# An attention and MLP kernel: where the gates' low halves, the operands' differences, the summary rows and the last batch's accumulators stand in the order of work

## The chip, the cores and the metric

The kernel runs on one core of one Trainium2 chip. The metric is device time in microseconds (us) of one execution. The engines are named as in the profile: PE is TensorE (matrix products), PEld its weight loads, DVE is VectorE, ACT is ScalarE, POOL is GpSimd, SP is SyncE, whose queue issues the transfers. Each engine works through its own instructions strictly in the order in which they were written; engines wait for one another through semaphores, which are set by what an instruction reads and writes.

## The reference

Two stages, for four batches of 768 tokens. First an attention with 8 heads of 64 channels, in which each token sees the keys within 16 places of it and one summary per block of 32 keys (the maximum of the keys; the mean of the values):

```python
k_sum = k.reshape(B, H, nb, block, D).max(axis=3)
v_sum = v.reshape(B, H, nb, block, D).mean(axis=3)
scores_all = concat(where(mask_l, scale * q @ k.T, -1e9),
                    scale * q @ k_sum.T + log(block))
a = softmax(scores_all)
attn = a @ concat(v, v_sum)
```

Then, with x the attention's output (4 x 768 x 512), a low-rank mixing over the tokens and an MLP with 2048 hidden units:

```python
u = x + ((x.T @ U) @ V).T
out = u + max(u @ w_ch1, 0) @ w_ch2
```

Everything is float32 at the interface, and U, V and the two weights come as float64 words.

## The kernel before

**Tiles and exactness.** The products run in TensorE's float32r form. To keep precision a value is split into a high half (a cast) and a low half (value less high half), and a product is three matmuls: high by high, high by low, low by high. The helper `split` (lines 184 to 187) does this: the cast is ScalarE's (line 186), the subtraction that of the engine named (line 187), mostly GpSimd for weights and VectorE for what lies in PSUM. An accumulator is one PSUM bank of 128 x 512 float32, and all tiles in PSUM come from one pool of eight banks (`bank`, line 99), taken in turn: a new tile waits until the last reader of the bank's earlier tile is done.

**Stages.** A start-up does the attention and mixing of batch 0 in an order written out as a list of words (`START`). The *first stage* is the MLP of batch 0: 16 blocks `f` of 128 hidden units, each in two halves of the tokens, with `up` (line 919), a gate (`up_out`, lines 931 and 932) and `down_rows` (line 941). It also turns the weights from float64 words, splits them, sums them for the later batches, and stores these. Beside it runs the attention of batch 1, cut into steps (`one_bank_steps`) that are laid on *places*: `place(i)` is called four times per block (i = 4f to 4f + 3), the steps are spread from place 6 to 64, and the dictionary `later` puts loads and the first key maxima on places 0 to 21. In one half of a block the order is: gate, `place`, transfers, split of the weights, weight sums, the summing of values on GpSimd, the products `down_rows` of the half before, the next `place`.

Batches 1 to 3 have two phases each. The *up phase* (`up_phase`, line 1200) computes the hidden units of pairs of blocks from seven operand tiles, after the manner of Strassen and Winograd, in 54 steps and two more that run in the down phase. The *down phase* (`down_phase`, line 1295) has 16 rows `f`; a row is six tiles of output: four of 128 channels by 512 tokens (tiles 0 to 3), then two that hold two channel groups by the last 256 tokens (tiles 4 and 5), three matmuls per tile or group. The attention of the next batch is spread over both phases: `later_steps`, 15 steps over the up phase, the rest over steps 0 to 90 of the down phase, one about every 3.6 tiles.

**Gates.** Before row f of the down phase the hidden row must be made into its gate: the high half gh = relu(h) on ScalarE (line 1269), the low half gl on VectorE (line 1270), from gh. Both have two buffers, so gh of row f + 1 can only be written when TensorE has read row f - 1. `gates(st, f + 1)` stands ahead of row f's first tile; for row 0 it stands four steps ahead of the up phase's end.

**Weights of the later batches.** `fetch_weight` loads a pair of units (SP's queue), `prepare` casts one unit on ScalarE and makes its low half on GpSimd, four units ahead of use; four ticks (one per step) after the second unit of a pair is prepared, the next load into that buffer is issued. In the down phase `prepare` stands behind a row's last tile.

**Operands.** `operands(st, i, k)`, k = 0 to 3, makes the operand tiles from the mixed rows: `mix_u` leaves a 128 x 384 tile in PSUM (lines 705 and 713); ScalarE copies it to `st.x` (line 739, "kept"); for k = 1 to 3 the tile is split into a B operand (lines 186 and 187, low half on VectorE), VectorE makes one or two differences from it (line 749, tiles `tmp`), and these are split into T operands (low half on GpSimd).

**Other lines that are named.** `key_maxima`: a maximum on VectorE (line 319) and four small copies (line 336), on ScalarE for batch 1. `value_summaries`: two copies of 24 summary rows into the value tile (line 340). The sum that they copy is made on GpSimd (`add_vsum`, lines 261 to 275). `scores` (354) and `scores_by_subtiles` (377); exponentials (403 and 413); `square_values` (494), the product with the values; `normalise` (506 to 508), which frees that product's bank; `turn_half` (463, 457).

**The end.** `leave` (line 1316, VectorE) adds the residual rows to an accumulator and sends the result (line 1326). In the last batch the last two rows are put in the order tile by tile, row 14 and row 15 of a tile together, and each of the two channel groups in tiles 4 and 5 leaves by itself.

Of the kernel before, what the change touches and what calls it, by code (L numbers as in the profile page):

```python
# [13 lines left out]
ALU = mybir.AluOpType  # L14
# [72 lines left out]
def body(ctx: ExitStack, tc, q0, q1, k, v, vn, uv, w1, w2, mask, ident, rep, out):  # L87
# [515 lines left out]
    def one_bank_steps(st):  # L603
# [20 lines left out]
        def turn(h, a):  # L624
# [3 lines left out]
            if a == 1 and h >= 2:  # L628
                summaries(h - 1)
# [99 lines left out]
    def operands(st, i, k):  # L729
# [355 lines left out]
    def do(items):  # L1085
# [12 lines left out]
        4: lambda: key_maxima(nxt, 0),  # L1098
# [167 lines left out]
    def gates(st, f):  # L1266
        h = st.h[f // 2][:, f % 2]
        gh, gl = gate_place("gh"), gate_place("gl")
        nc.scalar.activation(gh, h, AF.Relu)  # L1269
        nc.vector.scalar_tensor_tensor(gl, h, 0.0, f32(gh), ALU.max, ALU.subtract)  # L1270
        return gh, gl

    def down_phase(st, g):
# [8 lines left out]
        acc, got = [], {}  # L1282
        for f, n in order:
            if f not in got:
                got[f] = (use_weight("down", f), *g)
                g = gates(st, f + 1) if f + 1 < NF else None
# [3 lines left out]
            q0, q1 = (0, DM) if n < NC else (DM, S)  # L1290
            channels = (n,) if n < NC else (2 * (n - NC), 2 * (n - NC) + 1)
            for i, c in enumerate(channels):
                place = acc[n][:, i * (q1 - q0) : (i + 1) * (q1 - q0)]
                for j, (part_w, gt) in enumerate(((0, gh), (0, gl), (1, gh))):
# [6 lines left out]
                        skip_group_check=n >= NC,  # L1301
                    )
                if f == NF - 1 and (n < NC or i == 1 or st.b == B - 1):
# [163 lines left out]
```

## Time and profile before

| what | value |
|---|---|
| time, median of 3 runs | 660.5 us (659.4 to 660.81) |
| time of the profiled execution | 661.57 us |
| its span | 659.8 us, granted clock 0.999 |
| TensorE busy | 636.1 us, 96% |
| TensorE weight loads busy | 571.1 us, 87% |
| VectorE, ScalarE, GpSimd busy | 362.5, 354.9, 364.2 us |
| moved by transfers | 116.17 MB, 176 GB/s in the mean |

How to read what follows. A row of the *timeline* has the start and the duration in us, engine, line, operation, output and input tiles, shapes and a count, and in brackets the idle time of the engine ahead of it and what ended that ("<-"). Rows with a count over 1 are merged: the duration then goes from the first start to the last end. The *table of waits* has who waited at which line for whom, the total in us, how often, and the longest. A wait "for issue" is one for which the profile shows no releaser. A *window* row has, for a stretch of time, the busy time of each engine, then the granted clock of TensorE, the busy share of the transfer engines and GB/s. Matmuls overlap one another, and the ends of matmuls are modelled. The start-up ends near 56 us, the first stage near 224; the up phases of batches 1, 2 and 3 begin near 224, 378 and 528, their down phases near 291, 442 and 585.

### The profile page before, as it was taken

What the parts mean: (1) busy time and instruction counts of PE and PEld (TensorE: products, weight loads), DVE (VectorE), ACT (ScalarE), POOL (GpSimd) and SP (SyncE); (2) the same over time, 40 slices, a digit from 0 to 9 for tenths busy, and PEclk for the clock granted to TensorE, in tenths of its full rate; (3) what the DMA queues carried; (4) which work ended last, traced back from release to release, by engine and by line L of the source; (5) the groups of instructions that cost most, each with busy time, mean ns of one, the idle gap of its engine ahead of it and who ended that gap; (6) DMA issues with size and microseconds to landing.
All of it is one profiled execution on the core that took longest, in us unless ns stands there. A gap on an engine that the chain in (4) does not pass through costs nothing.

```text
span 659.8 us, 14400 instructions
## 1 busy us (share of the span) xinstructions
PE 636.1 (96%) x5436; PEld 571.1 (87%) x5436; DVE 362.5 (55%) x996; ACT 354.9 (54%) x795; POOL 364.2 (55%) x402
## 2 busy tenths in 40 slices
PE   5899999999999999999999999999999999999997
PEld 5779878989888899998888899998888899998885
DVE  5679767765767596566553645566544522232223
ACT  4765666656564557665453467765553555553320
POOL 5423977975585776862245775771243565653320
PEclk9999999999999999999999999999999999999999
DMA  8996588776676169895519177886423164341102
GB/s 218 246 365 198 164 272 267 203 216 201 186 249 193 50 202 297 238 273 164 167 53 254 64 239 231 250 268 188 140 62 96 31 223 139 112 127 65 33 1 95
DMA packets 76358, 116.17 MB, mean 176 GB/s; under 512 B 6912, under 2 KB 51328, under 8 KB 76288
## 3 DMA queue, kind: packets, MB, share of 16 engines
q1 hardware_dynamic: 76288, 115.24, 58.0%
q8 instruction: 43, 0.70, 0.4%
q14 instruction: 27, 0.22, 0.1%
HBM read 91.10 MB, written 24.12 MB: 175 GB/s over the span
## 4 chain that ended last, share of the span: by engine, by line
PE 82%; DVE 5%; ACT 5%; DMA 3%; issue 2%; POOL 1%; SPq 1%; ACTq 0%; DVEq 0%; POOLq 0%
PE acc L1295 28%; PE ps_h L1200 26%; PE acc L941 8%; PE ps_h L919 7%; PE ps_x L494 3%; DMA place<-in_v 2%; PE ps_s L377 2%; PE ps_s L354 2%; DVE gl L1270 1%; PE ps_t L463 1%; PE ps_u L705 1%; PE ps_m L671 1%; ACT op L186 1%; DVE tmp L749 1%; PE ps_x L480 1%
## 5 line engine op out<-in xcount | busy, mean ns | idle before, releaser
L187 POOL TENSOR_TENSOR parts<-whole,parts 128x512 fp32r<-128x512 f32 (+1 forms) x144 | 182.4, 1274 | 151.3 <-ACT parts L186 143.2
L1295 PE MATMUL acc<-gh,parts 128*128 128x256 f32 (+1 forms) x768 | 199.1, 341 | 1.3 <-DVE o L1316 1.0
L1200 PE MATMUL ps_h<-op,parts 128*128 128x384 f32 x1008 | 181.6, 337 | 0.1
L1200 PEld LDWEIGHTS ps_h<-op,parts 128*128 128x128 f32 x1008 | 174.2, 188 | 2.7 <-issue 1.1
L1295 PEld LDWEIGHTS acc<-gh,parts 128*128 128x128 f32 x768 | 132.9, 189 | 19.5 <-issue 1.7
L1295 PE MATMUL acc<-gl,parts 128*128 128x256 f32 (+1 forms) x384 | 130.3, 339 | 1.8 <-DVE gl L1270 1.6
L1270 DVE SCALAR_TENSOR_TENSOR gl<-place,gh 128x768 fp32r<-128x768 f32 x48 | 58.9, 1226 | 101.6 <-ACT gh L1269 101.6
L186 ACT CAST parts<-whole 128x512 fp32r<-128x512 f32 (+1 forms) x144 | 83.1, 583 | 2.5 <-DMA whole<-up 1.2
L1295 PEld LDWEIGHTS acc<-gl,parts 128*128 128x128 f32 x384 | 72.7, 189 | 10.5 <-DVE gl L1270 3.8
L413 ACT ACTIVATE e<-e,neg 128x120 f32<-128x120 f32 x144 | 46.5, 386 | 61.3 <-DVE neg L403 61.3
L919 PE MATMUL ps_h<-place 128*128 128x384 f32 x384 | 74.3, 341 | 0.0
L941 PE MATMUL acc<-place,gh 128*128 128x512 f32 x192 | 67.4, 406 | 1.3 <-POOL place L187 1.1
L1269 ACT ACTIVATE gh<-place 128x768 fp32r<-128x768 f32 x48 | 40.5, 845 | 51.8 <-PE acc L1295 51.8
L919 PEld LDWEIGHTS ps_h<-place 128*128 128x128 f32 x384 | 66.1, 188 | 1.5 <-issue 0.4
L162 POOL TENSOR_SCALAR val<-place 128x512 f32<-128x512 f32 (+1 forms) x30 | 48.2, 1621 | 21.9 <-ACT place L149 18.2
L187 POOL TENSOR_TENSOR place<-val,place 128x512 fp32r<-128x512 f32 x29 | 38.8, 1360 | 21.3 <-ACT place L186 21.3
L187 POOL TENSOR_TENSOR op<-tmp,op 128x384 fp32r<-128x384 f32 x24 | 25.7, 1079 | 43.3 <-ACT op L186 42.9
L941 PEld LDWEIGHTS acc<-place,gh 128*128 128x128 f32 x192 | 35.8, 188 | 9.9 <-POOL place L187 2.9
L403 DVE CUSTOM_DVE_ANT_0 e<-ps_s,mask_sb 128x120 f32<-128x120 f32 x144 | 32.7, 276 | 10.4 <-PE ps_s L354 5.9
L941 PE MATMUL acc<-place,gl 128*128 128x512 f32 x96 | 37.7, 393 | 0.0
L932 DVE SCALAR_TENSOR_TENSOR gl<-ps_h,gh 128x384 fp32r<-128x384 f32 x32 | 17.8, 555 | 29.4 <-ACT gh L931 29.3
L931 ACT ACTIVATE gh<-ps_h 128x384 fp32r<-128x384 f32 x32 | 15.7, 492 | 32.2 <-PE ps_h L919 32.1
(118 smaller groups left out, 824.4 us busy)
## 6 DMA issues: line engine op xcount, KB each, us to landing
place<-in_w SPq DMA_DIRECT2D x32, 512.0 KB, 5.8
whole<-up SPq DMA_DIRECT2D x24, 512.0 KB, 4.2
whole<-down SPq DMA_DIRECT2D x24, 512.0 KB, 4.2
whole<-up SPq DMA_DIRECT2D x24, 384.0 KB, 3.5
vt<-in_v SPq DMA_DIRECT2D x48, 146.2 KB, 3.7
kt<-in_k SPq DMA_DIRECT2D x24, 288.0 KB, 5.3
there<-squares SPq DMA_DIRECT2D x16, 384.0 KB, 4.2
at<-there SPq DMA_DIRECT2D x64, 96.0 KB, 3.4
```

The source lines that it names most:

```text
L162: nc.gpsimd.tensor_scalar(f32(bits), f32(hi), 0.0, None, ALU.mult)
L186: nc.scalar.copy(hi, val)
L187: engine.tensor_tensor(lo, val, f32(hi), ALU.subtract)
L403: nc.vector.tensor_tensor_reduce(out=e[:, u, :], in0=ps[:, i * KC : (i + 1) * KC], in1=mask_sb[:, m, :], scale=-SCALE, scalar=BIG, op0=ALU ...
L413: nc.scalar.activation(e[:, u, :], e[:, u, :], AF.Exp, bias=st.neg[h][:, u : u + 1], scale=-1.0,)
L494: nc.tensor.matmul(ps[32 * i : 32 * i + 32, u * DV : (u + 1) * DV], at[:KC, i, u], vt[u % 2][:, (u // 2) * 2 + (i // 2 + u) % 2], start=Tr ...
L919: nc.tensor.matmul(ps[:, :NH], w_split[0, f][:, c % 2, part_w, c // 2], ut[:, c, :], start=(n == 0), stop=(n == 3 * NC - 1),)
L941: nc.tensor.matmul(acc[t], gt[:, sl], w_split[1, f][:, part_w], start=(first and j == 0), stop=(last and j == 2),)
L1200: nc.tensor.matmul(ps, a[:, sa, i], b[:, sb, i], start=(first and n == 0), stop=(n == 5), skip_group_check=not first,)
L1269: nc.scalar.activation(gh, h, AF.Relu)
L1270: nc.vector.scalar_tensor_tensor(gl, h, 0.0, f32(gh), ALU.max, ALU.subtract)
L1295: nc.tensor.matmul(place, w[:, part_w, c * P : (c + 1) * P], gt[:, q0:q1], start=(f == 0 and i == 0 and j == 0), stop=(f == NF - 1 and j = ...
```

## The change

- **Gates.** `gates` is cut into `gate_high` (ScalarE) and `gate_low` (VectorE). The high half of row f + 1 stays ahead of row f's first tile; the low half is issued behind row f's second tile, ahead of the step that follows that tile. For row 0 the high half is issued eight steps ahead of the up phase's end and the low half six.
- **Preparation.** `prepare` in the down phase stands behind a row's third tile instead of its last.
- **Accumulators.** In the last batch tiles 4 and 5 become four tiles of 128 x 256, each in its own bank, so that eight accumulators are open. Its last two rows are ordered as the four wide tiles of row 14, those of row 15, the narrow tiles of row 14, those of row 15. `leave` is called once per tile, with no half of a bank left out; in batches 1 and 2 it does what it did.
- **Operands.** For k = 1 to 3 the high half is cast before the copy to `st.x`, and VectorE makes the differences before the B operand's low half.
- **Batch 1 in the first stage.** The summary rows of head 0 are written after head 1's second turn (place 13) instead of after head 2's second half of scores (place 16); the key maxima of head 0 stand on place 5 instead of 4.

The diff, cut to its core:

```diff
@@ one_bank_steps
-            if h == 2:
-                summaries(0)
...
-            if a == 1 and h >= 2:
+            if a == 1 and h >= 1:
                 summaries(h - 1)
@@ operands
-        nc.scalar.copy(kept, ps.rearrange("p (u q) -> p u q", q=P))
+        def keep():
+            nc.scalar.copy(kept, ps.rearrange("p (u q) -> p u q", q=P))
+        def high(name, val):
+            nc.scalar.copy(st.op[name][:, 0, i], val)
+        def low(name, val, engine):
+            t = st.op[name][:, :, i]
+            engine.tensor_tensor(t[:, 1], val, f32(t[:, 0]), ALU.subtract)
         def part(name, val):
-            t = st.op[name][:, :, i]
-            split(t[:, 0], t[:, 1], val, nc.vector if name[0] == "B" else nc.gpsimd)
+            high(name, val)
+            low(name, val, nc.gpsimd)
...
         if k == 0:
+            keep()
             st.tmp["B12"] = kept
-        elif k == 1:
-            part("B22", ps)
+            return
+        name = (None, "B22", "B11", "B21")[k]
+        high(name, ps)
+        keep()
+        if k == 1:
             st.tmp["T3"] = tmp()
             combine(st.tmp["T3"], ps, st.tmp["B12"], ALU.subtract)
+            low(name, ps, nc.vector)
             part("T3", st.tmp["T3"])
         elif k == 2:
-            part("B11", ps)
             st.tmp["T1"] = tmp()
             st.tmp["T2"] = tmp()
             combine(st.tmp["T1"], st.tmp["B12"], ps, ALU.subtract)
             combine(st.tmp["T2"], st.tmp["T3"], ps, ALU.add)
+            low(name, ps, nc.vector)
             part("T1", st.tmp["T1"])
             part("T2", st.tmp["T2"])
         else:
-            part("B21", ps)
             combine(st.tmp["T3"], ps, st.tmp["T2"], ALU.subtract)
+            low(name, ps, nc.vector)
             part("T4", st.tmp["T3"])
@@ later
-        4: lambda: key_maxima(nxt, 0),
+        5: lambda: key_maxima(nxt, 0),
@@ gates
-    def gates(st, f):
+    def gate_high(st, f):
         h = st.h[f // 2][:, f % 2]
         gh, gl = gate_place("gh"), gate_place("gl")
         nc.scalar.activation(gh, h, AF.Relu)
+        return h, gh, gl
+    def gate_low(h, gh, gl):
         nc.vector.scalar_tensor_tensor(gl, h, 0.0, f32(gh), ALU.max, ALU.subtract)
-        return gh, gl
@@ down_phase
+        whole = [[(c, 0, DM)] for c in range(NC)]
+        rest = [(c, DM, S) for c in range(NC)]
+        tiles_of_out = whole + ([rest[:2], rest[2:]] if st.b < B - 1 else [[x] for x in rest])
+        n_all = len(tiles_of_out)
-        order = [(f, n) for f in range(NF) for n in range(NU)]
+        order = [(f, n) for f in range(NF) for n in range(n_all)]
         if st.b == B - 1:
-            order[-2 * NU :] = sorted(order[-2 * NU :], key=lambda fn: (fn[1], fn[0]))
+            order[-2 * n_all :] = sorted(order[-2 * n_all :], key=lambda fn: (fn[1] >= NC, fn))
...
-                got[f] = (use_weight("down", f), *g)
-                g = gates(st, f + 1) if f + 1 < NF else None
+                got[f], seen[f] = (use_weight("down", f), *g[1:]), 0
+                g = gate_high(st, f + 1) if f + 1 < NF else None
...
-                if f == NF - 1 and (n < NC or i == 1 or st.b == B - 1):
-                    leave(st, acc[n], q0, q1, channels[: i + 1] if st.b < B - 1 else (c,), i)
+            if f == NF - 1:
+                leave(st, acc[n], q0, q1, [c for c, _, _ in tiles_of_out[n]])
+            seen[f] += 1
+            if seen[f] == 2 and g:
+                gate_low(*g)
             yield
-            if n == NU - 1:
+            if seen[f] == 3:
                 prepare()
@@ the loop over the up phase
-            if i == UP - 4:
-                g = gates(cur, 0)
+            if i == UP - 8:
+                g = gate_high(cur, 0)
+            if i == UP - 6:
+                gate_low(*g)
```

More of the change, by code (lines that the diff above doesn't have):

```diff
@@ L1289, in down_phase @@
                 acc.append(bank(f"acc{n}"))
[L1290 to L1292 removed]
+            for i, (c, q0, q1) in enumerate(tiles_of_out[n]):
                 place = acc[n][:, i * (q1 - q0) : (i + 1) * (q1 - q0)]
@@ L1300, in down_phase, with leave @@
                         stop=(f == NF - 1 and j == 2),
-                        skip_group_check=n >= NC,
+                        skip_group_check=len(tiles_of_out[n]) > 1,
                     )
-                if f == NF - 1 and (n < NC or i == 1 or st.b == B - 1):
-                    leave(st, acc[n], q0, q1, channels[: i + 1] if st.b < B - 1 else (c,), i)
+            if f == NF - 1:
[3 more added lines that the diff above has]
+                gate_low(*g)
             yield
-            if n == NU - 1:
+            if seen[f] == 3:
                 prepare()
-    def leave(st, acc, q0, q1, channels, i):
+    def leave(st, acc, q0, q1, channels):
         n = len(channels)
-        first = 0 if n > 1 else i
         o = mo.tile([P, DM], F32, name="o", tag="val", bufs=VALS)[:, : n * (q1 - q0)]
@@ L1317, in leave @@
                 o[:, part].rearrange("p (u q) -> p u q", q=P),
-                acc[:, (first + k) * (q1 - q0) : (first + k + 1) * (q1 - q0)].rearrange(
-                    "p (u q) -> p u q", q=P
-                ),
+                acc[:, part].rearrange("p (u q) -> p u q", q=P),
                 channel_rows(st, c)[:, q0 // P : q1 // P],
```

2 lines of the change are left out of this document (1 added, 1 removed).

## The prediction

> **What bounds the kernel now.** I read the profile page first, then TensorE's table of waits, then the timeline of all engines around each wait. From the page:
>
> ```profile
> span 659.8 us, 14400 instructions
> PE 636.1 (96%) x5436; PEld 571.1 (87%) x5436; DVE 362.5 (55%) x996; ACT 354.9 (54%) x795; POOL 364.2 (55%) x402
> ```
>
> TensorE is busy for 636.1 of 659.8 us and no other engine for more than 56%. The change takes no matmul away and adds none, so it can only win time in which TensorE waits, or that lies behind its last matmul. Next, therefore, the waits of TensorE alone (line and what it waited for; total, times, longest in us). I leave out those of the start-up, which the diff does not touch:
>
> ```profile
> PE ps_s L377 <- issue: 2.1, 4, 0.7
> PE acc L1295 <- DVE gl L1270: 1.6, 3, 0.6
> PE ps_x L494 <- ACT vt L340: 1.4, 2, 1.2
> PE acc L941 <- POOL place L187: 1.1, 2, 0.7
> PE acc L1295 <- DVE o L1316: 1.0, 2, 0.5
> PE ps_u L705 <- DVE tmp L749: 0.7, 1, 0.7
> PE ps_t L463 <- DVE tmp L749: 0.5, 1, 0.5
> PE acc L1295 <- ACT gh L1269: 0.2, 1, 0.2
> ```
>
> They sum to 8.6 us, but each place costs more than is listed, because the end of a matmul is drawn later than the next one could have started. The timeline at one place:
>
> ```profile
> 67.45 0.40 PE L941 MATMUL acc<-place,gl 128*128 128x512 f32 x1
> 68.31 0.73 PE L941 MATMUL acc<-place,gh 128*128 128x512 f32 x2 [0.46 <-POOL place L187]
> 69.12 0.62 PE L941 MATMUL acc<-place,gh 128*128 128x512 f32 x2
> ```
>
> An undisturbed pair takes 0.62 and one matmul 0.40, so starts are 0.22 to 0.23 apart. The matmul after 67.45 could have started at 67.68; it started at 68.31, which is 0.63 and not 0.46, and its pair takes 0.73, another 0.11. So a wait costs its listed idle plus 0.17 + 0.11 = 0.28 us.
>
> **The first stage: key maxima one place later, the first summary rows sooner.** What stands around these waits on ScalarE, VectorE and GpSimd:
>
> ```profile
> 62.99 1.28 DVE L171 SCALAR_TENSOR_TENSOR val<-place,val 128x512 int32<-128x512 int32 x2
> 65.30 0.95 ACT L336 COPY kt<-km 64x48 f32<-64x48 f32 x4 [2.24 <-DVE km L319]
> 66.28 1.14 ACT L186 CAST place<-val 128x512 fp32r<-128x512 f32 x2
> 66.55 0.82 PE L354 MATMUL ps_s<-kt,qz 128*128 128x120 f32 x6
> 66.98 2.53 POOL L187 TENSOR_TENSOR place<-val,place 128x512 fp32r<-128x512 f32 x2 [4.24 <-ACT place L186]
> 78.29 3.05 POOL L187 TENSOR_TENSOR place<-val,place 128x512 fp32r<-128x512 f32 x2
> 85.58 0.37 POOL L275 TENSOR_SCALAR vsum<-vsum 128x64 f32<-128x64 f32 x1
> 89.19 0.49 ACT L931 ACTIVATE gh<-ps_h 128x384 fp32r<-128x384 f32 x1 [1.67 <-PE ps_h L919]
> 97.65 1.06 ACT L340 COPY vt<-vsum 24x390 f32<-24x390 f32 x2
> ```
>
> The weight's values were ready at 62.99 + 1.28 = 64.27, but its cast stood on ScalarE behind four copies of key maxima, which had waited 2.24 for VectorE. At place 5 the copies stand behind the casts, VectorE's order being the same (nothing of VectorE's is issued between the two places for an odd block). The casts start at 64.3 instead of 66.28, so GpSimd's low half starts 2.0 sooner, at 65.0, and its first half-weight (2.53 / 2) is there at 66.2, ahead of 67.68: the wait at 68.31 goes. GpSimd then runs without a pause up to the low halves of 78.29; a start 2.0 sooner there covers the second of the two waits (0.7 listed, 1.0 with what hides) and the 0.7 us by which TensorE itself comes sooner, with 0.3 left over. The price: the key copies now end near 65.4 + 0.95 = 66.4, against scores that started at 66.55. Cost 0, and at most a few tenths if the casts slip.
>
> The summary rows are written at 97.65 and TensorE waits for them (1.4). They now come right behind the copies of head 1's second turn, near 87.5 (where ScalarE's idle ahead of the gate at 89.19 begins, 89.19 - 1.67), and their sum on GpSimd is ready by then (85.58 + 0.37 = 85.95). If it were late, ScalarE's gate at 89.19 and all behind it would wait; ScalarE idles 1.67 ahead of that gate, which covers the 1.06 of the copies. Saved: 1.1 + 1.4 listed at three places, + 3 x 0.28 = **3.3 us**.
>
> **Operands: differences ahead of low halves, the kept rows behind the high half.** Around the longest of these waits:
>
> ```profile
> 217.59 0.48 ACT L186 CAST op<-ps_u 128x384 fp32r<-128x384 f32 x1
> 218.10 0.56 DVE L187 TENSOR_TENSOR op<-ps_u,op 128x384 fp32r<-128x384 f32 x1 [1.86 <-ACT op L186]
> 219.04 0.55 DVE L749 TENSOR_TENSOR tmp<-tmp,ps_u 128x384 f32<-128x384 f32 x1
> ```
>
> TensorE next needs this PSUM bank, and its last reader ends at 219.59. Everything depends on whether VectorE may read the bank while ScalarE still does. If it may, the differences start with the first cast, the last read ends about 1 us sooner, and both waits for L749 go: 0.7 + 0.5 + 2 x 0.28 = 1.8 us. If not, VectorE starts where it does now (ScalarE's two reads only change places), runs the same two or three operations in another order and ends where it does now: 0. The trace has no two engines on one bank at once: VectorE's 218.10 follows the cast's end, 218.07, though there it needs its data. The Trainium skill, "PSUM — Partial Sum Buffer", section "PSUM bank collisions raise a hardware error", says that two engines must not touch one bank and quadrant at a time, reads against reads included, and that scheduling adds a dependency; by it the 1.8 us stay. The nearest row is the table's "DVE o L1316": TensorE waits there for VectorE's read of the other half of a bank, other addresses altogether. I take **0** and keep 1.8 for the range. Sure is only that the T operands are there one VectorE operation (about 0.5) sooner, which helps ScalarE's queue, next.
>
> **The gates and the weights' preparation in batches 1 and 2.** Two kinds of wait:
>
> ```profile
> 312.56 1.41 DVE L1270 SCALAR_TENSOR_TENSOR gl<-place,gh 128x768 fp32r<-128x768 f32 x1 [1.76 <-ACT gh L1269]
> 313.89 0.15 DVE L506 TENSOR_SCALAR sum<-ps_x 128x6 f32<-128x6 f32 x1
> 314.30 0.56 DVE L508 TENSOR_TENSOR x<-ps_x,sum 128x384 f32<-128x384 f32 x1
> 371.28 0.62 ACT L186 CAST parts<-whole 128x512 fp32r<-128x512 f32 x1
> 371.81 0.84 ACT L1269 ACTIVATE gh<-place 128x768 fp32r<-128x768 f32 x1
> ```
>
> At 312.56 VectorE has waited 1.76 for the gate's high half and then works 1.41, with the normalisation behind it in its queue. The scores that "waited for issue" (2.1) come just after that normalisation ends (314.30 + 0.56 = 314.86): they wait for the bank that it frees. Two of the four products stand right behind their row's first tile, and there the normalisation now precedes the low half: about 2 us sooner against a wait of 1.0. The other two stand behind the second tile, still behind the low half; there it helps that the weight's cast (0.62) no longer stands ahead of the gate on ScalarE, 0.5 against a listed 0.3. The waits for gl outside the tail go likewise: at 371.81 the gate loses the 0.53 in front of it, and 0.5 from the operands, against a listed 0.6 and 0.28. Saved: 2.1 + two thirds of 1.6 = 3.2 listed at six places, + 6 x 0.28 = 4.9.
>
> What is added: the low half now waits behind whatever VectorE does after the first tile, and TensorE needs it one row later. The tightest place has an operand step there:
>
> ```profile
> 343.90 2.01 DVE L1270 SCALAR_TENSOR_TENSOR gl<-place,gh 128x768 fp32r<-128x768 f32 x1 [0.32 <-ACT gh L1269]
> 344.54 0.48 ACT L186 CAST op<-ps_u 128x384 fp32r<-128x384 f32 x1
> 347.70 0.40 PE L1295 MATMUL acc<-gl,parts 128*128 128x512 f32 x1
> L1270 DVE SCALAR_TENSOR_TENSOR gl<-place,gh x48: 916/1112/2016, 290.0 to 646.5; 128x768 fp32r<-128x768 f32 x48
> ```
>
> ScalarE's reads end at 345.0, two VectorE operations of 0.55 at about 346.1; then gl, 0.92 (the shortest of 48, by the row of its line) to 2.01, ends between 347.0 and 348.1 against 347.70. Lost: 0 to 0.4 + 0.28, once in each of two batches, 0 to 1.4. I take 0.5, so **4.4 us** net. The preparation moved three steps up issues a cast, GpSimd's low half and, four ticks later, a load on SP's queue, ahead of outputs and later loads there. Its weight is used four rows later, about 4 x 4.2 = 17 us by the spacings below, so I cost it 0; were GpSimd 2 us late, SP would hold that load and what follows by as much. The gate of row 0 moved four up-steps sooner has no wait now: 0.
>
> **The tail.** Eight accumulators let the last two rows run as four whole tiles, four whole tiles, then the narrow ones, each in its own bank:
>
> ```profile
> 645.30 0.52 PE L1295 MATMUL acc<-gh,parts 128*128 128x256 f32 x2
> 656.48 0.29 PE L1295 MATMUL acc<-gh,parts 128*128 128x256 f32 x1
> 656.80 0.42 DVE L1316 TENSOR_TENSOR o<-acc,x 128x256 f32<-128x256 f32 x1 [0.72 <-PE acc L1295]
> out_t<-o SPq DMA_DIRECT2D x4, 128.0 KB, 1.7
> 654.00:655.00 1.00, 1.00 (x9) 1.00 (x10) 0.41 (x1) 0.00 (x0) 0.00 (x0) 1.00 0.85 321
> ```
>
> Row 14 starts at 645.30 + 0.52 - 0.40 = 645.42. Unbroken, its and row 15's 24 wide matmuls take 24 x 0.228 and the 24 narrow ones 24 x 0.12 (0.40 for a pair less 0.28): 8.35, so the last starts at 645.42 + 8.35 - 0.12 = 653.65 instead of 656.48, 2.8 sooner. Row 15 starts 2.7 behind row 14 instead of 0.7, time enough for its gate (0.84 as at 371.81, + 0.92 to 1.11); and the waits for gh, gl and o leave (0.2 + 0.5 + 1.0 + 4 x 0.28 = 2.8, the same by the other way). Narrow tiles end 0.36 apart and VectorE takes 0.42 for one, partly overlapped: up to 0.2 late. Outputs come at 256 KB per 3 x 0.228 us, 380 GB/s, where a busy microsecond shows 321: up to 0.5 late. At row 0 the eighth bank waits for the last sum of the up phase; its cover is three narrow steps of 0.36 against 0.32 + 0.55, at most a few tenths. I take **2.8**, lower end 2.0.
>
> **Sum.** 3.3 + 0 + 4.4 + 2.8 = 10.5 us. The profiled run took 661.57 (span 659.8 and 1.8 around it): 651.1. It is 1.1 above the median of the three runs shown, 660.5, against which the result is held: **650.0 us**.
>
> **Rivals.** (1) Both engines read a bank at once and the operands' waits go too: 648.2. For it: the two engines would only read. Against: the wait for L1316 and the page. (2) The first stage gives its gain back: GpSimd is busy there almost without a pause, and a sooner TensorE may meet the next low half instead. Then 653.3. For it: only 0.3 us were left over in the sum above. Against: TensorE's list has two such waits in all, so behind the second GpSimd keeps up by itself. (3) The waits are only replaced, each by the next late engine, and the tail alone is won: 657.7. Against: GpSimd, VectorE and ScalarE are each 55% busy. (4) Slower: the clock. TensorE without its pauses might be granted less than now. Each 1% costs 6.4 us of the 636, so from 1.65% on all is eaten; at 0.97 it would be 669. Against it stands the last up phase, where TensorE and its weight loads leave no gap and the clock is full:
>
> ```profile
> 550.00:560.00 10.00, 10.00 (x60) 10.00 (x59) 2.22 (x4) 4.97 (x11) 5.87 (x5) 1.00 0.50 147
> ```
>
> **How the numbers follow.** My forecast 0.60, (1) 0.15, (2) 0.15, (3) 0.06, (4) 0.04. The range: low, (1) with the 0.5 for the low half not lost and 1 us of scatter like that of the three runs (659.4 to 660.81), 646.5; high, (2) with half of the batches' gain, 653.3 + 2.4 = 655.7, taken as 655.5. A change under 0.2%, 1.3 us, can't be told from none. Only (4), and a failure of (3) in the tail as well, are not faster: faster 0.94, same 0.03, slower 0.03.
>
> **What would show it.** Right: TensorE's table of waits without "DVE o", "ACT gh", "POOL place" and "ACT vt", with "DVE tmp" still there; narrow L1316 some 0.36 apart at the end; the low halves without their idle on VectorE in batches 1 and 2. Wrong: L377 still waiting after a product, new waits for gl near the operand steps, or a clock under 0.99.

## The result, and the profile after

The changed kernel takes 649.99 us in the median (648.68 to 651.52) against 660.31 us (659.4 to 660.81) of the kernel before, measured beside it: a ratio of 0.9846, 95% interval 0.9821 to 0.9871, or 10.3 us less. The profiled execution took 649.63 us with a span of 647.8 and a granted clock of 1.0. First the page: the span, TensorE's and the other engines' busy times, and the shares of the chain that ended last.

```profile
span 647.8 us, 14395 instructions
PE 631.3 (97%) x5436; PEld 570.0 (88%) x5436; DVE 360.7 (56%) x996; ACT 356.2 (55%) x795; POOL 364.6 (56%) x402
PE 91%; DMA 4%; DVE 2%; ACT 2%; issue 1%; SPq 0%; DVEq 0%; ACTq 0%
```

The same 5436 matmuls are done, and VectorE, ScalarE and GpSimd have as much to do as before within 2 us. TensorE's 4.8 us less of "busy" are no less work either: 14 waits have left its table, and with each goes the 0.28 by which the ends around a wait are drawn late, an estimated 3.9 of the 4.8. What went is waiting. TensorE's table of waits, whole (what it waited for; total, times, longest):

```profile
PE ps_s L354 <- DVE place L336: 8.0, 1, 8.0
PE ps_s L354 <- DMA place<-in_q: 1.6, 1, 1.6
PE ps_n L293 <- DMA place<-in_v: 1.0, 2, 0.6
PE ps_t L463 <- DVE op L746: 0.7, 1, 0.7
PE ps_m L669 <- issue: 0.6, 1, 0.6
PE ps_u L703 <- DVE op L746: 0.5, 1, 0.5
PE ps_s L354 <- POOL place L340: 0.4, 1, 0.4
```

Behind the start-up only two are left, those of lines 463 and 703. They are the two waits for an operand's bank. Together they are as long as before, but that of line 463 was 0.5 and is 0.7, and the other was 0.7 and is 0.5. They have a new last reader: the B operand's low half (line 746) now reads the bank last, where a difference did.

How much was won where can be read from the starts of the matmuls, which are not modelled: both kernels issue 5436, so the n-th of one is set against the n-th of the other. Both begin at 8.01; the last starts at 656.48 before and at 644.14 after, 12.34 sooner. Cut at the 700th matmul (64 us), the 2200th (260 us, in batch 1's up phase), the 4800th (543 us, in batch 3's) and the last 48, the gain is

| stretch | changed kernel | forecast |
|---|---|---|
| start-up | 0.67 | 0 |
| first stage | 3.67 | 3.3 |
| batches 1 and 2 | 4.95 | 4.4 |
| batch 3 up to the last 48 matmuls | 0.21 | 0 |
| last 48 matmuls | 2.84 | 2.8 |

From 12.34, 0.34 is lost again behind the last matmul (656.48 to the span's end at 659.8 before, 644.14 to 647.8 after). The start-up, which the diff does not touch, is scatter: over the thirteen changed kernels of this study it ended between 1.77 later and 1.51 sooner than in the profiled run of before. The waits for first loads differ there (1.6 for `in_q` in the table above), and in three runs (gates and preparation alone, order alone, changed without the gates' split) the granted clock is 0.72 to 0.76 between 33 and 39 us, where it is 1.00 before. The profiled run of before was also 0.6 to 1.3 above the medians of its kernel (660.31 to 660.99), so that 11.9 us between the two profiled runs go with 10.3 between the medians.

The stages, in the changed kernel's timeline. The first stage:

```profile
63.69 1.14 ACT L186 CAST place<-val 128x512 fp32r<-128x512 f32 x2 [1.31 <-DVE val L171]
64.39 2.98 POOL L187 TENSOR_TENSOR place<-val,place 128x512 fp32r<-128x512 f32 x2 [2.33 <-ACT place L186]
64.74 0.95 ACT L336 COPY kt<-km 64x48 f32<-64x48 f32 x4
...
83.12 0.37 POOL L275 TENSOR_SCALAR vsum<-vsum 128x64 f32<-128x64 f32 x1
85.30 1.05 ACT L340 COPY vt<-vsum 24x390 f32<-24x390 f32 x2
```

The casts run ahead of the key copies, GpSimd's low half starts at 64.39 instead of 66.98, and the summary rows are written at 85.30, behind a sum that was ready at 83.49. An operand step:

```profile
169.21 0.47 ACT L742 CAST op<-ps_u 128x384 fp32r<-128x384 f32 x1
169.58 0.49 ACT L739 COPY x<-ps_u 128x384 f32<-128x384 f32 x1
170.16 0.55 DVE L756 TENSOR_TENSOR tmp<-x,ps_u 128x384 f32<-128x384 f32 x1 [1.61 <-ACT x L739]
...
171.09 0.55 DVE L746 TENSOR_TENSOR op<-ps_u,op 128x384 fp32r<-128x384 f32 x1
...
171.79 0.52 PE L463 MATMUL ps_t<-ident_sb,e 128*120 128x128 f32 x3 [0.70 <-DVE op L746]
...
175.82 0.56 DVE L756 TENSOR_TENSOR tmp<-ps_u,tmp 128x384 f32<-128x384 f32 x1 [1.47 <-ACT x L739]
```

VectorE's difference starts behind ScalarE's second read, the copy to `st.x`. At 170.16 its other input is an earlier row of that same tile `x`, so that this row alone does not show what it waits for. At 175.82 its inputs are the bank and a `tmp` that VectorE itself made at 170.63, and still it waits for the copy: only the bank is left to order the two. A product in batch 1, then the tail:

```profile
306.35 0.17 DVE L506 TENSOR_SCALAR sum<-ps_x 128x6 f32<-128x6 f32 x1 [1.58 <-PE ps_x L494]
...
308.14 1.94 DVE L1285 SCALAR_TENSOR_TENSOR gl<-place,gh 128x768 fp32r<-128x768 f32 x1
309.13 0.85 PE L377 MATMUL ps_s<-kt,qz 64*64 64x120 f32 x24
...
639.54 2.73 DVE L1336 TENSOR_TENSOR o<-acc,x 128x512 f32<-128x512 f32 x4 [1.59 <-PE acc L1313]
643.38 1.50 DVE L1336 TENSOR_TENSOR o<-acc,x 128x256 f32<-128x256 f32 x4 [1.10 <-PE acc L1313]
644.14 0.28 PE L1313 MATMUL acc<-gh,parts 128*128 128x256 f32 x1
```

The normalisation precedes the low half, and line 377's 24 matmuls run without a break. At the end four sums take 1.50, so they start (1.50 - 0.42) / 3 = 0.36 apart, each right behind its tile.

### The profile page after: what moved, and what is told of

It is laid out like the page before. It is cut to its first block, busy times and chain, and to the rows that moved or that the text cites. A ratio compares the mean times of both kernels' runs of the same rounds, so it can differ in the third digit from the quotient of the medians.

```text
span 647.8 us, 14395 instructions
## 1 busy us (share of the span) xinstructions
PE 631.3 (97%) x5436; PEld 570.0 (88%) x5436; DVE 360.7 (56%) x996; ACT 356.2 (55%) x795; POOL 364.6 (56%) x402
## 4 chain that ended last, share of the span: by engine, by line
PE 91%; DMA 4%; DVE 2%; ACT 2%; issue 1%; SPq 0%; DVEq 0%; ACTq 0%
PE acc L1313 31%; PE ps_h L1212 27%; PE acc L953 10%; PE ps_h L931 9%; PE ps_x L494 3%; PE ps_s L354 3%; PE ps_s L377 2%; DMA place<-in_q 2%; PE ps_u L703 2%; DMA qz<-in_q 1%; PE ps_t L463 1%; PE ps_m L669 1%; PE ps_u L711 1%; PE ps_x L480 1%; PE ps_r L687 1%
## 5 line engine op out<-in xcount | busy, mean ns | idle before, releaser
L1285 DVE SCALAR_TENSOR_TENSOR gl<-place,gh 128x768 fp32r<-128x768 f32 x48 | 55.2, 1149 | 71.5 <-ACT gh L1281 71.4
L168 DVE SCALAR_TENSOR_TENSOR val<-place,val 128x512 int32<-128x512 int32 (+1 forms) x33 | 32.0, 972 | 3.1 <-POOL val L162 3.0
L1238 DVE TENSOR_TENSOR place<-place,ps_h 128x384 f32<-128x384 f32 x24 | 13.2, 550 | 36.8 <-PE ps_h L1212 36.8
```

The costliest lines, as they stand in the source:

```text
L168: lambda lo, hi, bits: nc.vector.scalar_tensor_tensor(bits, lo, 29, bits, ALU.logical_shift_right, ALU.bitwise_or),
```

## The experiments

The same cut of the matmuls' starts, for every kernel run; gains in us against the profiled run of before, behind the start-up. A stretch that a kernel leaves as it was differs by up to 0.23, nearly all of it at one matmul of the first stage (90.34 in the kernel before). In two runs one transfer came late in batch 1: TensorE's tables have "ps_x L494 <- DMA at<-there" with 0.4 in the tail alone and 0.7 in the order alone, which is their -0.32 and -0.75.

| run | ratio, 95% interval | first stage | batches 1, 2 | batch 3 | last 48 |
|---|---|---|---|---|---|
| tail alone | 0.9962 [0.9948, 0.9976] | 0.23 | -0.32 | 0.02 | 2.84 |
| first stage alone | 0.9943 [0.9925, 0.9960] | 3.39 | 0.03 | -0.01 | -0.04 |
| gates and preparation alone | 0.9942 [0.9922, 0.9962] | 0.19 | 3.17 | 0.21 | -0.02 |
| operands alone | 0.9964 [0.9951, 0.9977] | 0.24 | 1.73 | 0.00 | -0.01 |
| order alone | 0.9986 [0.9972, 0.9999] | 0.23 | -0.75 | 0.00 | 1.29 |
| low half alone | 0.9974 [0.9963, 0.9985] | 0.19 | 1.91 | 0.21 | -0.02 |
| preparation alone | 0.9953 [0.9935, 0.9971] | 0.03 | 3.11 | 0.00 | 0.00 |
| key maxima alone | 0.9975 [0.9959, 0.9991] | 1.70 | -0.03 | 0.00 | 0.00 |
| changed, without the gates' split | 0.9853 [0.9830, 0.9876] | 3.67 | 5.01 | -0.01 | 2.84 |
| changed, all reads from the copy | 0.9853 [0.9836, 0.9870] | 4.05 | 4.07 | 0.21 | 2.84 |
| changed, cast and low half from the copy | 0.9804 [0.9783, 0.9826] | 5.43 | 5.39 | 0.21 | 2.84 |
| changed, cast from the copy | 0.9797 [0.9774, 0.9819] | 4.77 | 5.71 | 0.21 | 2.84 |

The four parts alone sum to 2.77 + 3.37 + 3.55 + 1.96 = 11.65 us in these starts, the whole change has 3.67 + 4.95 + 0.21 + 2.84 = 11.67: what is won is kept to the end.

In batches 1 and 2, though, two parts overlap, and that their sums agree is a coincidence. By the starts around each place, the whole change wins 3.22 there at the four waits of line 377, 0.95 at the two listed waits for gl (373.85 and 524.31 in the kernel before), and 0.74 at two more waits for gl (337.64 and 488.12) that are listed on the weight load alone. The first of these, in the kernel before:

```profile
337.64 0.19 PEld L1295 LDWEIGHTS acc<-gl,parts 128*128 128x128 f32 x1 [0.47 <-DVE gl L1270]
```

Gates and preparation alone win the 3.22 and the 0.74, and lose 0.84 at four places that wait for gl. The operands alone win 0.99 at the listed waits for gl and the same hidden ones, 0.78. So the hidden gain is counted twice, and a loss that comes only without the operands' new order makes up for it.

**The tail alone.** Eight accumulators and the new order of the last two rows, nothing else.

```diff
-            order[-2 * NU :] = sorted(order[-2 * NU :], key=lambda fn: (fn[1], fn[0]))
+            order[-2 * n_all :] = sorted(order[-2 * n_all :], key=lambda fn: (fn[1] >= NC, fn))
...
+            for i, (c, q0, q1) in enumerate(tiles_of_out[n]):
```

> Only the eight accumulators and the order of the last two rows; the rest as before. Theory of own waits (each part takes away its own waits and TensorE keeps the time): 2.8 us less, ratio 0.9958; the waits for gh, gl and o behind 645 us are gone, the last two rows take 8.35 us from first to last start, the narrow sums stand 0.36 to 0.42 apart. Rival (the outputs are the bound at the end): the last matmul comes 2.8 sooner but the span ends 2.0 sooner or less.

The last 48 matmuls come 2.84 sooner, and the waits for gh, for o and for gl in the tail are gone. The 2.8 of the forecast is the gain up to the last matmul; 0.4 of it goes again behind it (the span, 657.3, ends 3.7 behind the last matmul's start instead of 3.3).

**The first stage alone.**

```diff
-            if h == 2:
-                summaries(0)
...
-            if a == 1 and h >= 2:
+            if a == 1 and h >= 1:
...
-        4: lambda: key_maxima(nxt, 0),
+        5: lambda: key_maxima(nxt, 0),
```

> Only the key maxima at place 5 and the first summary rows at place 13. Own waits: 3.3 us less, ratio 0.995; the waits of TensorE for L187 and L340 are gone from its table and those for L749 stand. Rival (the first stage gives it back, GpSimd being busy there without a pause): 0.7 to 1.5 us less, with a new wait for a low half of L187 between 75 and 130 us.

3.39 in the first stage, and nothing of it is given back in the batches (0.03, -0.01, -0.04).

**Gates and preparation alone.** The low half is issued behind a row's second tile, but behind the first tile of row 14 in the last batch, where the old order of the tail needs it.

```diff
-                g = gates(st, f + 1) if f + 1 < NF else None
+                g = gate_high(st, f + 1) if f + 1 < NF else None
...
+            if seen[f] == (1 if st.b == B - 1 and f == NF - 2 else 2) and g:
+                gate_low(*g)
...
-            if n == NU - 1:
+            if seen[f] == 3:
                 prepare()
```

> Only the gates' two halves issued apart, row 0 four steps sooner, and the preparation behind the third tile; for the last batch's row 15 the low half is issued behind row 14's first tile, since the tail's order is still the old one. Own waits: 4.0 to 4.9 us less, ratio 0.993; the scores no longer wait for issue, the waits for gl outside the tail nearly gone. Rival (the low half now comes late behind the operand steps): 2.5 us less or fewer, with waits for gl at the rows that have an operand step.

The waits of line 377 are gone, and batches 1 and 2 win 3.17 us in all. But the waits for gl in batches 1 and 2, which the forecast counted here, stay and grow. TensorE's table of this run, and one of those places:

```profile
PE acc L1298 <- DVE gl L1273: 2.0, 3, 0.8
```

```profile
369.89 2.00 POOL L187 TENSOR_TENSOR op<-tmp,op 128x384 fp32r<-128x384 f32 x2 [0.60 <-ACT op L186]
370.18 0.84 ACT L1269 ACTIVATE gh<-place 128x768 fp32r<-128x768 f32 x1
371.05 1.65 DVE L1273 SCALAR_TENSOR_TENSOR gl<-place,gh 128x768 fp32r<-128x768 f32 x1 [1.33 <-ACT gh L1269]
```

The gate does come sooner, since no weight's cast stands ahead of it; but the low half now runs beside GpSimd's low halves of the T operands and takes 1.65, where the shortest of its kind takes 0.92. The preparation alone has the same 2.0 in its table and the low half alone 1.5, so it is the preparation's move that lengthens these waits.

**Operands alone.**

```diff
+        high(name, ps)
+        keep()
+        if k == 1:
             st.tmp["T3"] = tmp()
             combine(st.tmp["T3"], ps, st.tmp["B12"], ALU.subtract)
+            low(name, ps, nc.vector)
             part("T3", st.tmp["T3"])
```

> Only the operands: high half ahead of the kept copy, differences ahead of low halves. Reads of one bank by two engines one after the other: the differences begin when ScalarE's second read ends, TensorE's two waits for VectorE (0.7 and 0.5) stay, only named after the low half instead of the difference; 0 to 0.9 us less, from gates that stand 0.5 sooner on ScalarE at the end of two batches. Reads side by side: the differences begin with the cast, both waits go, 1.8 to 2.7 us less.

Both bank waits stay, 0.7 at line 463 and 0.5 at line 705, with the low half as their last reader, and still 1.73 us are won in batches 1 and 2. Of the waits for gl in TensorE's table only the tail's is left (0.5, once): the T operands are cast one VectorE operation sooner, and with them the gate behind them in ScalarE's queue. This is the forecast's "one VectorE operation (about 0.5) sooner, which helps ScalarE's queue". Each of the two listed waits gives 0.48 and 0.51, less than listed idle plus 0.28, because some 0.4 of it stays on the weight load; the two hidden ones give 0.39 each. The 0.24 in the first stage belongs to the operands too: -0.24 and 0.29 at the two bank waits and 0.18 at one place between.

**All reads from the copy.** The changed kernel with ScalarE's copy to `st.x` first; cast, differences and low half then all read this copy, and the bank has one reader.

```diff
+        keep(ps)
+        ps = kept
         high(name, ps)
-        keep()
```

> The changed kernel, and ScalarE's copy to x comes first; high halves, differences and low halves then read that copy instead of the PSUM bank, so the bank has one reader, 0.48 us. Reads of one bank go one after the other, and TensorE waits for the bank: its two waits behind the operands (0.7 and 0.5, with 0.28 each 1.8) go, 8.5 to 12 us less than before in all. Rival: VectorE's operations now have both inputs in SBUF and are slowed beside GpSimd, as gl is (0.92 alone, up to 2.0); operations of 0.55 take up to 1.1, the T operands and the gates behind them come later, new waits for gl; no gain on the changed kernel or a loss of up to 1 us.

Both waits at the bank go, which shows that the readers one after another were what held it. But the time is that of the changed kernel. From TensorE's table of this run, then its timeline at a step like the one shown above:

```profile
PE ps_h L932 <- DVE gl L945: 1.1, 1, 1.1
PE acc L1314 <- DVE gl L1286: 1.1, 2, 0.6
```

```profile
167.75 2.85 POOL L187 TENSOR_TENSOR place<-val,place 128x512 fp32r<-128x512 f32 x2 [1.05 <-ACT place L186]
...
169.38 1.64 DVE L756 TENSOR_TENSOR tmp<-tmp,x 128x384 f32<-128x384 f32 x1
```

The difference, 0.55 long with one input in PSUM, takes 1.64 with both in SBUF: it ends at 171.02, 0.42 behind GpSimd's low halves (167.75 + 2.85 = 170.60), as if it had been let through only then. VectorE falls behind, and new waits for gl take what the bank gave. The Trainium skill, "SBUF — State Buffer", section "SBUF: two separate sides", says that a VectorE operation with two inputs in SBUF and a GpSimd operation share a pair of ports, when the GpSimd operation reads SBUF as well, and that the one that comes second is held for the whole instruction of the first; the 1.64 and the 1.65 above agree with it, and so does the 0.55 that an operation with one input in PSUM keeps beside the same GpSimd work (169.31 against 168.28 in the last timeline of this section).

**Order alone.** The kernel before with only the order of the last two rows, on six accumulators.

```diff
-            order[-2 * NU :] = sorted(order[-2 * NU :], key=lambda fn: (fn[1], fn[0]))
+            order[-2 * NU :] = sorted(order[-2 * NU :], key=lambda fn: (fn[1] >= NC, fn))
```

> The kernel before with the last two rows in the changed order, six accumulators as before. Own waits: the waits for gh and gl of row 15 go, 0.2 + 0.5 + 2 x 0.28 = 1.3 us less; the two for the sums of half a bank (o) stay. Rival (eight banks do it all): nothing changes by more than 0.3.

1.29 of the tail's 2.84: the waits for gh and gl go, that for o (1.0 at two places, 1.56 with what hides) stays, since two groups still share a bank. The eight accumulators are worth the other 1.55.

**Low half alone** and **preparation alone**: the two halves of "gates and preparation", each in the kernel before. The first has the split of that run with `prepare` behind the sixth tile as before; the second is

```diff
-            if n == NU - 1:
+            if seen[f] == 3:
                 prepare()
```

> Only the gates' low half later (and row 0 sooner), the preparation where it was; row 15's low half behind row 14's first tile. Own waits: of the four waits of the scores the two long ones (0.7, behind a first tile) go, the two short ones (0.3, behind a second tile) stay: about 2.0 less. Rival (the preparation's move does the work): no change.

> Only the preparation behind the row's third tile, the gates whole as before. Own waits: the two short waits of the scores (0.3) go, the long ones shrink from 0.7 to about 0.2, the gates at the end of two batches come 0.5 sooner: 1.5 to 2.5 less. Rival (it is the low half's place alone): no change.

The low half alone ends the two long waits of line 377 and leaves the two short ones (0.6 in all): 1.91. The preparation alone ends all four: 3.11, more than was expected of it, and at each place of batches 1 and 2 within 0.03 what gates and preparation together give. The place that the prediction shows and the row ahead of it, first in the kernel before, then with the preparation alone:

```profile
306.07 0.60 ACT L186 CAST parts<-whole 128x512 fp32r<-128x512 f32 x1
306.58 0.84 ACT L1269 ACTIVATE gh<-place 128x768 fp32r<-128x768 f32 x1
306.76 1.29 POOL L187 TENSOR_TENSOR parts<-whole,parts 128x512 fp32r<-128x512 f32 x1 [1.94 <-ACT parts L186]
307.46 1.41 DVE L1270 SCALAR_TENSOR_TENSOR gl<-place,gh 128x768 fp32r<-128x768 f32 x1 [1.97 <-ACT gh L1269]
...
310.42 0.89 PE L494 MATMUL ps_x<-vt,at 120*32 120x65 f32 x48
311.69 0.84 ACT L1269 ACTIVATE gh<-place 128x768 fp32r<-128x768 f32 x1
```

```profile
304.84 0.83 ACT L1269 ACTIVATE gh<-place 128x768 fp32r<-128x768 f32 x1
305.71 0.96 DVE L1270 SCALAR_TENSOR_TENSOR gl<-place,gh 128x768 fp32r<-128x768 f32 x1 [1.45 <-ACT gh L1269]
...
309.22 0.89 PE L494 MATMUL ps_x<-vt,at 120*32 120x65 f32 x48
309.49 0.84 ACT L1269 ACTIVATE gh<-place 128x768 fp32r<-128x768 f32 x1
...
312.96 0.85 PE L377 MATMUL ps_s<-kt,qz 64*64 64x120 f32 x24
```

Without the cast the gate is 0.5 sooner; and without GpSimd's low half of the weight beside it, the gate's low half takes 0.96 instead of 1.41. Together that is 0.95 on VectorE, and what follows in the queues comes that much sooner against TensorE: the next gate starts 0.27 behind the product's first matmul (309.49 against 309.22) instead of 1.27. The long wait was 0.7 + 0.28.

**Changed, without the gates' split.** High and low half stand together ahead of the row's first tile again, for row 0 four steps ahead of the up phase's end.

```diff
                 g = gate_high(st, f + 1) if f + 1 < NF else None
+                if g:
+                    gate_low(*g)
...
-            if seen[f] == 2 and g:
-                gate_low(*g)
```

> The changed kernel with the gates' split taken back: the low half is issued right behind the high half again, ahead of the row's first tile, for row 0 four steps ahead of the up phase's end. Theory, after the runs of parts: the preparation's move alone ended the waits of the scores behind a product, and the operands' new order those for gl at the batches' ends, so that the split is worth next to nothing beside them: within 0.7 us of the changed kernel (ratio 0.984 to 0.986), with no wait of line 377 over 0.3. Rival, that of the prediction: the low half ahead of the normalisation makes the scores wait where a product stands behind a row's first tile: one wait of 0.6 or more in each of two batches comes back, 2 x (0.6 + 0.28) = 1.8 us or more, ratio 0.987 or above.

The waits of line 377 stay away. VectorE idles 92.7 us ahead of its low halves, against 71.4 in the changed kernel, and TensorE loses nothing by it but the 0.21 of batch 3. That is row 0's gate, for which the weight load waits in the kernel before, with nothing of it on the matmul's side:

```profile
584.89 0.19 PEld L1295 LDWEIGHTS acc<-gl,parts 128*128 128x128 f32 x1 [0.30 <-DVE gl L1270]
```

Beside the other parts the gates' split is thus worth 0.2 us.

**Key maxima alone.**

```diff
-        4: lambda: key_maxima(nxt, 0),
+        5: lambda: key_maxima(nxt, 0),
```

> The kernel before with only the key maxima of head 0 moved from place 4 to place 5. Theory: this alone lets the weight's cast go ahead of the key copies, so both waits for GpSimd's low half (line 187: 1.1 listed at two places) go and that for the summary rows (1.4) stays or grows a little: 1.1 + 2 x 0.28 = 1.7 us less than the kernel before, ratio 0.9975. Rival: TensorE comes sooner to the summary rows, which are written when they were, so the gain is lost at that place: its wait grows from 1.4 to about 2.5 and the time is that of the kernel before.

1.70, of which 0.76 and 0.79 come at the two waits for line 187, and 0.2 at the matmul of 90.34 that moves in runs without this edit too. In its table of waits the summary rows' wait stays as it was:

```profile
PE ps_x L494 <- ACT vt L340: 1.4, 2, 1.2
```

Of the first stage's 3.39 the rows' move has thus the other 1.69 (1.67 at its own matmul), where the listed 1.4 + 0.28 is 1.68. The rival falls: the rows themselves came sooner, at 94.43 instead of 97.65, 1.45 of it by the start-up and the rest with TensorE.

**Two ways to free the bank sooner.** Both begin with the copy; the cast reads the copy, the differences go on reading the bank. In the first the low half also reads the copy, in the second it reads the bank.

```diff
-        high(name, ps)
         keep()
+        high(name, kept)
...
-            low(name, ps, nc.vector)
+            low(name, kept, nc.vector)
```

(the last two lines in the first kernel alone)

> The changed kernel, with ScalarE's copy of the operands' rows first; the cast of the high half and VectorE's low half then read that copy, while VectorE's differences go on reading the PSUM bank. So the bank has one reader of ScalarE (about 0.48 us) and then the differences. Theory: what holds the bank is that the reads of ScalarE and VectorE come one after another; both waits at the bank (0.7 and 0.5 listed, 0.28 more each) go, and the kernel takes about 1.3 to 1.8 us less than the changed one, a ratio of 0.981 to 0.983 to the kernel before. Rival: the low half, which now has both inputs in SBUF, is slowed beside GpSimd as in the run in which all reads but the copy's were taken from SBUF (0.55 becomes 0.65 to 0.95), the gates' low halves behind it come later, and new waits for gl take back what the bank gave: 0.984 to 0.986.

> The changed kernel, with ScalarE's copy of the operands' rows first; only the cast of the high half reads that copy. VectorE's differences and low half read the PSUM bank as before, so no operation of VectorE has both of its inputs in SBUF that had not before. Theory: VectorE can start as soon as the copy is done instead of behind cast and copy, about 0.4 us sooner. The wait of 0.7 listed shrinks to about 0.3, that of 0.5 to about 0.1, no new wait for gl comes: 0.8 us less than the changed kernel in all, a ratio near 0.983. Rival: the low half needs the cast, which now comes last, and the bank is freed when it was: no change, 0.9845.

Both are faster than either kernel: medians of 647.43 and 646.94 us, 2.6 and 3.1 below the changed kernel's; by the starts 2.2 and 1.9. The kernel without the split, on the same chip, took 650.39. From the second one's timeline:

```profile
168.28 2.54 POOL L187 TENSOR_TENSOR place<-val,place 128x512 fp32r<-128x512 f32 x2 [1.05 <-ACT place L186]
...
168.74 0.48 ACT L739 COPY x<-ps_u 128x384 f32<-128x384 f32 x1
169.25 0.52 ACT L742 CAST op<-x 128x384 fp32r<-128x384 f32 x1
169.31 0.55 DVE L756 TENSOR_TENSOR tmp<-x,ps_u 128x384 f32<-128x384 f32 x1 [1.35 <-issue]
...
170.94 0.51 PE L463 MATMUL ps_t<-ident_sb,e 128*120 128x128 f32 x3
```

The cast (from the copy) and the difference (from the bank) now run at once. The two bank waits give 0.55 and 0.38, and 0.2 more comes a few us behind the first. The rest comes by ScalarE's casts of the T operands, as in the operands alone: the groups of that line in the changed kernel, then in this one (count, busy time and mean of one, idle time before them and what ended it):

```profile
L742 ACT CAST op<-tmp 128x384 fp32r<-128x384 f32 x24 | 12.0, 513 | 12.1 <-DVE tmp L756 12.1
```

```profile
L742 ACT CAST op<-tmp 128x384 fp32r<-128x384 f32 x24 | 12.0, 514 | 3.2 <-DVE tmp L756 1.6
```

Idle time of 12.1 us shrinks to 3.2, the gates behind these casts come sooner, and what was left of the waits for gl at the ends of batches 1 and 2 goes (0.39 and 0.35 by the starts). In the changed kernel it shows in the weight loads alone: it hid behind a matmul's late-drawn end.

```profile
PEld acc L1313 <- DVE gl L1285: 0.8, 2, 0.4
```

The expectation of 0.8 us for this kernel counted the bank only, and was too small. Between the two kernels the runs don't decide: the first frees the bank sooner but its low half takes 0.63 in the mean instead of 0.55.

## Why the prediction came out, step by step

**The bound.** TensorE's order of matmuls, so only waits and the tail could be won: right. No engine's work changed, the clock stayed (rival 4 falls), and the gain is the sum of the waits.

**Listed idle plus 0.28 for each wait.** Right to about 0.1 where a wait was taken away whole, measured at its own matmuls: line 187's waits 1.1 + 2 x 0.28 = 1.66, measured 1.55; the summary rows 1.68, measured 1.67; line 377 2.1 + 4 x 0.28 = 3.2, measured 3.22. At the bank, with all reads from the copy, it is 0.98 and 0.78 against 0.88 and 0.65 measured. The two waits for gl, 1.1 + 2 x 0.28 = 1.66, gave 0.95 in the changed kernel, where 0.4 of each stays on the weight load, and 1.69 with the cast from the copy, where that goes too. And the rule can't see a wait that is listed on the weight load alone: two such gave 0.74.

**The first stage, 3.3.** Right in mechanism and size, 3.39 alone. Rival 2, that the stage gives its gain back, falls.

**The operands, 0.** The reason was right: VectorE does not read the bank while ScalarE does, so the waits there stay and rival 1 falls. The table has "DVE tmp L756 <- ACT x L739", 26.4 us in 16 places, and in four of these (inputs `ps_u` and `tmp`, as at 175.82) nothing but the bank orders the two. The Trainium skill's rule that the prediction weighed ("PSUM — Partial Sum Buffer", section "PSUM bank collisions raise a hardware error") agrees with this; what would come of reads at once no run shows. But the term was mis-sized: alone, the operands won 1.73 in batches 1 and 2 instead of 0. What failed is the step "The waits for gl outside the tail go likewise", which put them under the gates and the preparation, by "the 0.53 in front of it, and 0.5 from the operands". The runs showed that the first does not help (the waits for gl grew from 1.6 to 2.0 in all with gates and preparation alone) and that the operands' half ends what TensorE's table lists, with 0.4 at each place left on the weight load.

**Gates and preparation, 4.9 less 0.5.** The sum of batches 1 and 2 is 4.95; of it, 3.2 belong here, 0.95 to the operands, and 0.74, the hidden waits for gl, to either. The 4.9 counted the whole of the listed waits for gl and nothing of the hidden ones, so that its closeness to 4.95 is luck in part. Three sub-steps were off. The product places behind a row's first tile were given to the low half's move; it does end their waits, but the preparation's move does so without it. The forecast took of that move only "0.5 against a listed 0.3" and missed that it also takes GpSimd's low half from beside the gate's, which shortens the latter from 1.41 to 0.96. The gate of row 0, costed at 0, brought 0.21. And the 0.5 for the low half behind an operand step was not lost: at that place in the changed kernel gl takes 0.95, not up to the 2.01 that the bound allowed.

**The tail, 2.8.** 2.84 up to the last matmul; the output's "up to 0.5 late" was 0.34, which the value taken had left out. VectorE's last sum follows the last matmul as it did, so the "up to 0.2 late" there was nothing.

**The sum.** 10.5 forecast, 10.3 between the medians. That closeness is partly luck: the terms were 1.5 us too small in sum against the spans of the two profiled runs (12.0 shorter), 0.37 in the first stage, 0.55 + 0.21 in the batches and 0.67 of start-up scatter, less 0.3 in the tail, and against the medians the scatter takes it back: the profiled run of before lay 1.3 above its median, that of after 0.4 below. Rival 3 falls, since no wait took another's place. Of the signs named, the four kinds of wait left the table and the narrow sums stand 0.36 apart; the bank's waits stayed, but under the low half's name instead of "DVE tmp". One sign came only in part: ahead of the low halves VectorE still idles 27.1 us in batches 1 and 2, of 54.0 before. The run without the gates' split, with more such idle time and no loss in these batches, shows that it says nothing about the time.

## What to carry to other kernels

A wait on the critical engine is worth its listed idle plus what the drawn end of the matmul hides, and the weight loads have waits that the matmuls do not list; but assign each wait to its cause by the chain behind it, since an engine's queue carries a small gain (here 0.5 on ScalarE from the operands) to a wait that looks like another edit's, and compare parts place by place, since two errors can make a sum agree. When an instruction is moved, ask what it runs beside as well as what it stands ahead of. Where two engines read one PSUM bank, try to let the one that can make a copy read it once and first, and leave the other's operations their one PSUM input: here that brought 1.9 us by the starts.

## What the runs showed of the hardware

VectorE's gate low half, with both inputs in SBUF, takes 0.92 to 0.96 us in the kernel before where GpSimd is idle when it starts (23 of 48). In the other 25 an operation of GpSimd was running, and the low half ends 0.81 to 0.82 us behind the end of that operation, however long it had run already: it takes 1.1 to 2.0 (at 307.46 above 1.41, from GpSimd's end at 308.05 to 308.87). The 128 x 384 difference takes 0.55 with an input in PSUM but 0.73 to 0.95 in the mean of its groups (1.64 at one place) with both in SBUF. Replacing a PSUM source by an SBUF copy is therefore not free, even where it frees a bank: with every read moved, the 0.88 and 0.65 won at two banks were lost again in new waits for gl.
